# Row sums of the masked exponentials: from VectorE's mask to ScalarE's conversion

## The chip, the core and the metric

The kernel runs on one core of a Trainium2 chip. Its engines are TensorE (PE in the profile, with its weight loads as PEld), VectorE (DVE), ScalarE (ACT), GpSimd (POOL) and SyncE (SP), which issues most of the transfers. Each engine takes its instructions strictly in the order in which the program holds them, and waits in front of one until its semaphores allow it. The metric is the time of one execution in microseconds, as the median of several runs.

## The reference, cut to what matters

There are 4 batches of 576 tokens. Attention with 8 heads of 64 comes first: for each query only the 32 largest scores are kept, and the softmax is taken over those. After it stand a gated mixer and an FFN with a Fourier mix, both of width 512.

```python
scores = scale * np.matmul(q, k.transpose(0, 1, 3, 2))
kth = np.partition(scores, -32, axis=-1)[..., -32:-31]
scores = np.where(scores >= kth, scores, -1e9)
attn = np.exp(scores - np.max(scores, axis=-1, keepdims=True))
attn = attn / (np.sum(attn, axis=-1, keepdims=True) + 1e-09)
x = np.matmul(attn, v)                       # then heads side by side: [4, 576, 512]
val = (sigmoid(causal_conv(x, conv_w)) * (x @ w_val)) @ w_out
u = val + np.real(fft(fft(val, axis=1), axis=2))
out = u + np.maximum(layernorm(u) @ w_ch1, 0) @ w_ch2
```

The change touches `np.sum(attn)`: where the row sums of the 32 kept exponentials are added up.

## The kernel before, in words

**Attention.** The work is cut into 4 batches (blocks) of 4 head pairs, and each head pair into 5 tiles of queries: u = 0 to 3 hold 128 queries of both heads (two halves, i = 0 and 1), and u = 4 holds the last 64 queries of both heads in one half. That makes 80 tiles and 144 halves of 128 rows by 576 keys. For each tile PE makes the scores (`pss`, line 219), ACT copies them to SBUF (`ssb`, lines 220 and 221), and DVE finds the 32nd largest value of each row: it folds the row by maxima and minima (lines 245 to 249), then takes four rounds of MAX8 (line 260) over 96, 144, 288 and 576 columns, with MATCH_REPLACE8 (line 269) after each of the first three. ACT makes the exponentials `e` meanwhile (line 265).

**The mask.** `mask()` for a half is not run in its own tile but inside the next tile's sequence, between that tile's folds and its four rounds. On DVE one instruction (line 283) multiplies `e` by (score >= threshold) in place, and by `accum_out` also gives the row sum into a column of `sums`. Then ACT writes the fp16 high part of `e` into `hl` (line 284), POOL or (in block 0) PE and ACT make the low part (lines 285 to 292), SP issues a transposing DMA from `hl` to `et` (line 294), and PE multiplies `et` with the values into `pav` (line 316, 28 matmuls for a full tile). `hl` has two buffers and `et` four.

**The end of a head pair.** `attn_finish` turns the nine columns of `sums` into reciprocals `rs` (DVE lines 334 and 335), splits them into fp16 parts `rsh` (ACT line 337, POOL line 338), spreads them over a tile by 20 small matmuls (`pr` and `pt`, lines 345 and 350), copies that to `xt` (ACT lines 353 and 354) and multiplies `pav` by `xt` (DVE line 355). There are 16 head pairs.

**The other work.** While the attention of block b runs, the mixer and the FFN of block b - 1 run beside it as units (`moe_units`): `pv` (line 407) are the gate's value matmuls, `ph` (line 579) and `po` (lines 602 and 617) the two FFN layers. `po` of the last 64 tokens (line 617) is called po_4 below. The units of the last block have no attention beside them, and run after it. In block 0 the weights are unpacked instead (lines 671 to 699). The order on each engine is set by a planner: the program is written as one stream, and a simulated timeline with its own costs for every instruction decides which ready instruction comes next on each engine; scores and a few others have a higher priority. So a changed instruction shifts the order of others as well.

Of the kernel before, what the change touches and what calls it, by code (L numbers as in the profile page):

```python
# [12 lines left out]
AF = mybir.ActivationFunctionType  # L13
ALU = mybir.AluOpType
# [3 lines left out]
B, H, S, D = 4, 8, 576, 64  # L18
# [42 lines left out]
def mixer_pass(  # L61
# [17 lines left out]
    act = nc.scalar.activation  # L79
    vec = nc.vector  # L80
# [142 lines left out]
    def ordered(prev):  # L223
        if prev is None:
            return nullcontext()
        return tc.issue_after(prev.ins if hasattr(prev, "ins") else prev)

    def attn_tiles(b, hp, u):
        st = state[("at", b, hp)]
        g = 2 if u < 4 else 1  # L230
        cols = [u, 5 + u] if u < 4 else [4]
        sel = slice(u, u + 6, 5) if u < 4 else slice(4, 5)
        y = ap.tile([P, 2, S], F32, tag="ty", name=f"ty_{b}_{hp}_{u}", bufs=1)
        ngm = ap.tile([P, 2], F32, tag="ngm", name=f"ngm_{b}_{hp}_{u}", bufs=4)
        ssb, pss = st.pop(("s", u))
        c = st["c"]
        todo = deferred.pop("mask", [])
        last = deferred.get("last")

        if viol is not None:  # L240
            lo, hi = pss[:, :g, 0:HS], ssb[:, :g, HS:S]
            m2a = pss[:, 2, P : P + g * QS].rearrange("p (g n) -> p g n", g=g)
            m2b = y[:, :g, HS : HS + QS]
            with ordered(last):
                vec.tensor_tensor(m2a, lo[:, :, 0:QS], hi[:, :, 0:QS], op=ALU.max)
            vec.tensor_tensor(m2b, lo[:, :, QS:HS], hi[:, :, QS:HS], op=ALU.max)
            vec.tensor_tensor(y[:, :g, 0:QS], m2a, m2b, op=ALU.max)
            vec.tensor_tensor(y[:, :g, QS:HS], m2a, m2b, op=ALU.min)
            last = vec.tensor_tensor(y[:, :g, HS:S], lo, hi, op=ALU.min)  # L249
            rounds = ((y, slice(0, FS)), (y, slice(0, QS)), (y, slice(0, HS)), (y, slice(0, S)))  # L250
        else:
            al = slice(0, S)
            rounds = ((ssb, al), (y, al), (y, al), (y, al))
        for f in todo:
            last = f(last)
        es = []
        for r, (src, w) in enumerate(rounds):
            for i in range(g):
                with ordered(last):
                    last = vec.max(out=c[:, cols[i], 8 * r : 8 * r + 8], in_=src[:, i, w])  # L260
            if r == 0:
                nc.scalar.mul(ngm[:, :g], c[:, sel, 0:1].rearrange("p g n -> p (g n)"), -SC_EXP)
                for i in range(g):
                    e = ap.tile([P, S], F32, tag="e", name=f"e_{b}_{hp}_{u}_{i}", bufs=3)
                    act(e, ssb[:, i, :], AF.Exp, bias=ngm[:, i : i + 1], scale=SC_EXP)  # L265
                    es.append(e)
            if r < 3:
                for i in range(g):
                    vec.match_replace(  # L269
                        out=y[:, i, w],  # L270
                        in_to_replace=c[:, cols[i], 8 * r : 8 * r + 8],
                        in_values=src[:, i, w],
                        imm_value=-1e30,
                    )
        deferred["last"] = last

        def mask(i, prev):
            e = es[i]
            hl = ap.tile([P, 2 * S], F16, tag="hl", name=f"hl_{b}_{hp}_{u}_{i}", bufs=2)
            thr = c[:, cols[i], 31:32]  # L280
            rsum = st["sums"][:, cols[i] : cols[i] + 1]
            with ordered(prev):
                done = vec.scalar_tensor_tensor(e, ssb[:, i, :], thr, e, op0=ALU.is_ge, op1=ALU.mult, accum_out=rsum)  # L283
            act(hl[:, 0:S], e, AF.Copy, bias=0.0, scale=1.0)  # L284
            pool.tensor_tensor(hl[:, S : S + D], e[:, 512:S], hl[:, 512:S], op=ALU.subtract)  # L285
            if b == 0:
                pe = ps_m.tile([P, 512], F32, tag="psm", name=f"pe_{hp}_{u}_{i}")
                mm(pe, eye, e[:, 0:512], start=True, stop=False)  # L288
                mm(pe, neye, hl[:, 0:512], start=False, stop=True)
                act(hl[:, S + D : 2 * S], pe, AF.Copy, bias=0.0, scale=1.0)  # L290
            else:
                pool.tensor_tensor(hl[:, S + D : 2 * S], e[:, 0:512], hl[:, 0:512], op=ALU.subtract)  # L292
            et = ap.tile([P, 9, P], F16, tag="et", name=f"et_{b}_{hp}_{u}_{i}", bufs=4)
            nc.sync.dma_start_transpose(et, hl)
            st[("et", u, i)] = et
            if viol is not None and u == 4:
                vec.tensor_reduce(c[:, :, 0:1], c[:, :, 7:24:8], axis=mybir.AxisListType.X, op=ALU.min)
                vs = viol[:, b * NPAIR + hp]
                pool.tensor_tensor(vs, c[:, :, 31], c[:, :, 0], op=ALU.subtract)
            return done  # L300

        deferred["mask"] = [lambda prev, i=i: mask(i, prev) for i in range(g)]

    def attn_av(b, hp, u):
# [667 lines left out]
```

## Time and profile before

| what | us |
|---|---|
| median of 3 runs (1051.89 to 1061.42) | 1057.13 |
| the profiled execution, own time | 1057.91 |
| its span, first to last instruction | 1054.4 |

The profile is of one execution. Busy times are of instructions alone, and an engine's idle time is put down to what ended it. A row of the timeline can stand for several merged instructions (x2); then its length is that of all of them. Two neighbours on one engine overlap in the record: the next one begins some tens of ns before the record of the one ahead has ended, so the distance between two starts is what an instruction takes of its engine. A trace row names a tile without its buffer or index; in the order lists below, `pr_3_11979` is the tile pr of head pair 3 with a running number behind, `et_3_4_0` is of head pair 3, tile u = 4, half 0.

### The profile page before, as it was taken

The page shows a single profiled execution, that of the slowest core. Times are in us where ns is not written, and L with a number is a line of the kernel's source. Part 1 is how long each engine was busy: PE and PEld are TensorE (multiplying, and loading weights), DVE is VectorE, ACT ScalarE, POOL GpSimd, SP SyncE. Part 2 cuts the span into 40 slices and gives each one's busy share as a digit, 9 for nine tenths or more (in the row PEclk, how much of TensorE's full clock was granted, in tenths as well). Part 3 has the DMA queues.
Part 4 walks back from the last instruction along what each step waited for, and adds up shares of the span by engine and source line. Part 5 has one row for each costly group of instructions (what it writes and reads, how often), then busy time and mean ns, then how long its engine had stood idle before and what let it go on. Part 6 is the DMA issues. An engine that isn't in the chain of part 4 may idle for free.

```text
span 1054.4 us, 21240 instructions
## 1 busy us (share of the span) xinstructions
PE 881.2 (84%) x7282; PEld 513.4 (49%) x7282; DVE 846.2 (80%) x2568; ACT 664.3 (63%) x1394; POOL 565.4 (54%) x806
## 2 busy tenths in 40 slices
PE   1277767866789799898998998979979998899996
PEld 0033233322455565544656555446555564558563
DVE  5987979968898999998899998999998997223120
ACT  5587987868756877766669758565785763323020
POOL 1764652524485766755957658559584663641000
PEclk9977888988999999998999999999989999999999
DMA  7698585766536555555364546664464353301000
GB/s 205 162 269 222 128 189 129 181 109 131 103 63 105 97 113 120 100 125 123 82 122 93 116 97 110 138 141 70 99 111 91 83 108 55 80 21 26 21 2 29
DMA packets 308805, 115.18 MB, mean 109 GB/s; under 512 B 297040, under 2 KB 300880, under 8 KB 306384
## 3 DMA queue, kind: packets, MB, share of 16 engines
q1 hardware_dynamic: 303840, 90.24, 43.8%
q10 hardware_dynamic: 4848, 23.50, 6.8%
q8 instruction: 59, 0.97, 0.4%
q14 instruction: 58, 0.48, 0.2%
HBM read 44.49 MB, written 6.82 MB: 49 GB/s over the span
## 4 chain that ended last, share of the span: by engine, by line
DVE 32%; PE 27%; ACT 14%; DMA 12%; issue 6%; POOL 6%; SPq 2%; ACTq 0%; POOLq 0%; DVEq 0%
DVE e L283 7%; PE ph L579 6%; DMA et<-hl 5%; PE po L602 5%; DVE tc L260 5%; DVE ty L269 4%; PE pv L407 3%; DMA stk<-pre 3%; DVE ty L249 2%; POOL hl L292 2%; PE pav L316 2%; ACT hl L284 2%; ACT ssb L220 2%; ACT e L265 2%; PE pd L461 2%
## 5 line engine op out<-in xcount | busy, mean ns | idle before, releaser
L260 DVE MAX8 tc<-ty 128x8 f32<-128x96 f32 (+3 forms) x576 | 229.8, 432 | 2.5 <-DVE e L283 0.5
L579 PE MATMUL ph<-R_un,w 128*128 128x256 f16 (+1 forms) x1536 | 202.3, 290 | 14.0 <-ACT bx_h L583 6.5
L579 PEld LDWEIGHTS <-w 128*128 128x128 f16 x1536 | 148.4, 99 | 62.8 <-issue 21.0
L219 PE MATMUL pss<-stk 128*128 128x512 f16 (+3 forms) x640 | 95.0, 306 | 74.3 <-DVE ty L249 45.0
L284 ACT ACTIVATE hl<-e 128x576 f16<-128x576 f32 x144 | 97.9, 683 | 92.6 <-DVE e L283 70.0
L283 DVE SCALAR_TENSOR_TENSOR e<-ssb,tc,e 128x576 f32<-128x576 f32 x144 | 139.4, 996 | 2.6 <-ACT e L265 2.4
L269 DVE MATCH_REPLACE8 ty<-tc,ty 128x144 f32<-128x144 f32 (+2 forms) x432 | 137.2, 323 | 0.0
L602 PE MATMUL po<-w2f,bx_h 128*128 128x512 f16 x576 | 129.2, 379 | 0.0
L316 PE MATMUL pav<-et,vhl 128*64 128x128 f16 (+1 forms) x2240 | 95.2, 224 | 38.7 <-DMA et<-hl 36.9
L292 POOL TENSOR_TENSOR hl<-e,hl 128x512 f16<-128x512 f32 x108 | 125.0, 1157 | 0.0
L265 ACT ACTIVATE e<-ssb,ngm 128x576 f32<-128x576 f32 x144 | 107.4, 777 | 3.9 <-PE pe L288 1.4
L316 PEld LDWEIGHTS <-vhl 128*64 128x64 f16 x2240 | 72.1, 115 | 77.1 <-issue 72.7
L285 POOL TENSOR_TENSOR hl<-e,hl 128x64 f16<-128x64 f32 x144 | 47.5, 333 | 104.6 <-ACT hl L284 82.3
L163 POOL TENSOR_TENSOR pre<-r,pre 96x384 f16<-96x384 f32 x60 | 60.7, 1020 | 79.5 <-ACT r L162 66.8
L219 PEld LDWEIGHTS <-stk 128*128 128x128 f16 (+1 forms) x640 | 41.4, 104 | 124.3 <-issue 76.2
L602 PEld LDWEIGHTS <-bx_h 128*128 128x128 f16 x576 | 55.1, 98 | 64.9 <-issue 0.6
L220 ACT COPY ssb<-pss 128x1024 f32<-128x1024 f32 (+1 forms) x80 | 73.4, 918 | 10.4 <-PE pss L219 7.9
L580 ACT ACTIVATE bx_h<-ph 128x256 f16<-128x256 f32 (+1 forms) x96 | 38.7, 409 | 55.4 <-PE ph L579 55.2
L407 PE MATMUL pv<-xhl,R_wv 128*128 128x288 f16 x384 | 55.9, 303 | 13.1 <-ACT xt L353 5.0
L156 ACT ACTIVATE pre<-r 96x384 f16<-96x384 f32 x60 | 29.6, 519 | 44.6 <-DMA stk<-pre 16.5
L249 DVE TENSOR_TENSOR ty<-pss,ssb 128x576 f32<-128x576 f32 (+1 forms) x80 | 55.6, 695 | 1.9
L697 PE MATMUL pl<-bx_pre,U_wp 128*128 128x512 f32 x72 | 45.4, 716 | 12.0 <-ACT hl L290 6.4
(186 smaller groups left out, 1705.3 us busy)
## 6 DMA issues: line engine op xcount, KB each, us to landing
bx_pre<-in_moe_w_ch_dram ACTq DMA_DIRECT2D x8, 1024.0 KB, 5.7
bz_pre<-in_moe_w_ch_dram ACTq DMA_DIRECT2D x8, 1024.0 KB, 5.3
r<-in_q_dram SPq DMA_DIRECT2D x32, 144.0 KB, 2.7
r<-in_k_dram SPq DMA_DIRECT2D x31, 144.0 KB, 2.6
stk<-stk SPq DMA_DIRECT2D x60, 72.0 KB, 2.3
vr<-in_v_dram SPq DMA_DIRECT2D x32, 128.0 KB, 2.7
out_dram<-U_u SPq DMA_DIRECT2D x16, 256.0 KB, 2.4
R_wv<-scr_wv SPq DMA_DIRECT2D x3, 1024.0 KB, 5.1
```

The source lines that it names most:

```text
L219: mm(pss[pr, bank, cs], stk[:, 2 * vv, qs], stk[:, 1, ks], start=(vv == 0), stop=(vv == 1))
L220: nc.scalar.copy(ssb[:, :g, 0:512], pss[:, :g, :])
L260: last = vec.max(out=c[:, cols[i], 8 * r : 8 * r + 8], in_=src[:, i, w])
L265: act(e, ssb[:, i, :], AF.Exp, bias=ngm[:, i : i + 1], scale=SC_EXP)
L269: vec.match_replace(out=y[:, i, w], in_to_replace=c[:, cols[i], 8 * r : 8 * r + 8], in_values=src[:, i, w], imm_value=-1e30,)
L283: done = vec.scalar_tensor_tensor(e, ssb[:, i, :], thr, e, op0=ALU.is_ge, op1=ALU.mult, accum_out=rsum)
L284: act(hl[:, 0:S], e, AF.Copy, bias=0.0, scale=1.0)
L292: pool.tensor_tensor(hl[:, S + D : 2 * S], e[:, 0:512], hl[:, 0:512], op=ALU.subtract)
L316: av = mm(st["pav"][i * D : (i + 1) * D, qs], vhl[:, hv, i, cv, :], rhs, start=(m == 0), stop=(m == len(steps) - 1),)
L407: mm(pv[:, :HS], a, r, start=(n == 0), stop=(n == len(pairs) - 1))
L579: mm(ph[:, :nt], a, r, start=(i == 0), stop=(i == len(pr) - 1))
L602: mm(po, a, r, start=(f == 0 and i == 0), stop=(f == NF - 1 and i == 2))
```

## The change

The mask on DVE no longer has an accumulator output, and the conversion on ACT that follows it has one, into the same column of `sums`. What is summed is the same masked `e`. The line that reads `sums` (334) now waits for ACT.

```diff
             with ordered(prev):
-                done = vec.scalar_tensor_tensor(e, ssb[:, i, :], thr, e, op0=ALU.is_ge, op1=ALU.mult, accum_out=rsum)
-            act(hl[:, 0:S], e, AF.Copy, bias=0.0, scale=1.0)
+                done = vec.scalar_tensor_tensor(e, ssb[:, i, :], thr, e, op0=ALU.is_ge, op1=ALU.mult)
+            act(hl[:, 0:S], e, AF.Copy, bias=0.0, scale=1.0, accum_out=rsum)
             pool.tensor_tensor(hl[:, S : S + D], e[:, 512:S], hl[:, 512:S], op=ALU.subtract)
```

The order moves at many places. The first shown is DVE at the end of a head pair (block 1, head pair 1), from the mask of its last tile to the reciprocal. Before:

```order
L283 SCALAR_TENSOR_TENSOR e_1_4_0_4010,sums_1_2734<-ssb_1_4_3790,tc_1_2733,e_1_4_0_4010 128x576
L260 MAX tc_2_3643<-ty_2_0_4109 128x8 x2
L334 TENSOR_SCALAR rs_1_2735<-sums_1_2734 128x9
L269 MATCH_REPLACE ty_2_0_4109<-tc_2_3643,ty_2_0_4109 128x96 x2
L335 RECIPROCAL rs_1_2735<-rs_1_2735 128x9
L260 MAX tc_2_3643<-ty_2_0_4109 128x8 x2
```

and now:

```order
L283 SCALAR_TENSOR_TENSOR e_1_4_0_4010<-ssb_1_4_3790,tc_1_2733,e_1_4_0_4010 128x576
L260 MAX tc_2_3643<-ty_2_0_4109 128x8 x2
L269 MATCH_REPLACE ty_2_0_4109<-tc_2_3643,ty_2_0_4109 128x96 x2
L260 MAX tc_2_3643<-ty_2_0_4109 128x8
L334 TENSOR_SCALAR rs_1_2735<-sums_1_2734 128x9
L260 MAX tc_2_3643<-ty_2_0_4109 128x8
L269 MATCH_REPLACE ty_2_0_4109<-tc_2_3643,ty_2_0_4109 128x144
L335 RECIPROCAL rs_1_2735<-rs_1_2735 128x9
```

The line that reads the sums (334) has moved three instructions back, behind the second round's replacements and one MAX8 of 144 columns; the same move is made at most of the 16 head pairs.

The second place is PE at the end of the last head pair of block 3, where no more attention follows. Weight loads are left out, and of each run of matmuls into one tile the first stands. Before:

```order
L316 MATMUL pav_3_11702<-et_3_1_1_11642,vhl_3_10836 64x128
...
L345 MATMUL pr_3_11979<-neye,rsh_3_11976 64x128
...
L350 MATMUL pt_3_11996<-neye,rsh_3_11976 64x64
...
L617 MATMUL po_4_12015<-w2f,bx_h_10107 64x512
...
L316 MATMUL pav_3_11702<-et_3_2_0_11755,vhl_3_10836 64x128
...
L617 MATMUL po_4_12015<-w2f,bx_h_10107 64x512
...
L316 MATMUL pav_3_11702<-et_3_2_1_11762,vhl_3_10836 64x128
...
L617 MATMUL po_4_12015<-w2f,bx_h_10107 64x512
...
L316 MATMUL pav_3_11702<-et_3_3_0_11861,vhl_3_10836 64x128
...
L617 MATMUL po_4_12015<-w2f,bz_h_10457 64x512
...
L407 MATMUL pv_0_0_12074<-xhl_0_9997,R_wv_12068 128x288
```

and now:

```order
L316 MATMUL pav_3_11702<-et_3_1_0_11635,vhl_3_10836 64x128
...
L316 MATMUL pav_3_11702<-et_3_2_0_11755,vhl_3_10836 64x128
...
L316 MATMUL pav_3_11702<-et_3_3_0_11861,vhl_3_10836 64x128
...
L345 MATMUL pr_3_11979<-neye,rsh_3_11976 64x128
...
L350 MATMUL pt_3_11996<-neye,rsh_3_11976 64x64
...
L617 MATMUL po_4_12015<-w2f,bx_h_10107 64x512
...
L345 MATMUL pr_3_11979<-neye,rsh_3_11976 64x128
...
L316 MATMUL pav_3_11702<-et_3_4_0_11885,vhl_3_10836 64x64
...
L617 MATMUL po_4_12015<-w2f,bx_h_10107 64x512
...
L407 MATMUL pv_0_0_12074<-xhl_0_9997,R_wv_12068 128x288
```

Before, `pr` stood ahead of the last three tiles' `pav`, and the 48 matmuls of po_4 between them. Now the `pav` of u = 1, 2 and 3 come in one piece, `pr` behind them, then 9 matmuls of po_4, the rest of `pr`, the `pav` of u = 4, and only behind that the other 39 of po_4 and all 96 matmuls of `pv`. The first `pav` of this head pair now stands behind 37 matmuls of po_3 and not 44.

## Rows read from the trace of the kernel before

**Rows 1.** The page: busy time of the engines, and the chain that ended last by engine.

```profile
PE 881.2 (84%) x7282; PEld 513.4 (49%) x7282; DVE 846.2 (80%) x2568; ACT 664.3 (63%) x1394; POOL 565.4 (54%) x806
...
DVE 32%; PE 27%; ACT 14%; DMA 12%; issue 6%; POOL 6%; SPq 2%; ACTq 0%; POOLq 0%; DVEq 0%
```

**Rows 2.** Busy us by stretch: length, engines (instructions), clock, DMA share, GB/s.

```profile
750.00:850.00 100.00, 89.79 (x881) 57.74 (x879) 94.79 (x315) 73.48 (x172) 65.23 (x94) 0.97 0.50 94
850.00:890.00 40.00, 38.87 (x334) 21.65 (x333) 38.58 (x120) 22.14 (x49) 18.14 (x27) 1.00 0.32 73
...
960.00:1054.00 94.00, 86.44 (x555) 51.76 (x552) 16.61 (x35) 11.80 (x28) 1.75 (x3) 0.98 0.05 16
```

**Rows 3.** Groups by form on DVE: shapes, count | busy us, mean ns | idle.

```profile
L283 DVE SCALAR_TENSOR_TENSOR e<-ssb,tc,e 128x576 f32<-128x576 f32 x144 | 139.4, 996 | 2.6 <-ACT e L265 2.4
...
L369 DVE SCALAR_TENSOR_TENSOR e<-pav,cw,e 128x574 f32<-128x574 f32 x16 | 12.9, 804 | 0.1
...
L283 DVE DVE_READ_ACCUMULATOR e<-ssb,tc,e 128x1 f32 x144 | 11.5, 80 | 0.0
```

**Rows 4.** Instructions on DVE in order of time: start, length, engine, line, operation.

```profile
405.81 0.80 DVE L369 SCALAR_TENSOR_TENSOR e<-pav,cw,e 128x574 f32<-128x574 f32 x1
406.53 0.51 DVE L260 MAX8 tc<-ty 128x8 f32<-128x144 f32 x2
...
412.95 0.76 DVE L249 TENSOR_TENSOR ty<-pss,ssb 128x576 f32<-128x576 f32 x1
413.63 0.81 DVE L283 SCALAR_TENSOR_TENSOR e<-ssb,tc,e 128x576 f32<-128x576 f32 x1
414.36 0.08 DVE L283 DVE_READ_ACCUMULATOR e<-ssb,tc,e 128x1 f32 x1
414.36 0.82 DVE L283 SCALAR_TENSOR_TENSOR e<-ssb,tc,e 128x576 f32<-128x576 f32 x1
```

**Rows 5.** The conversion as a group by form on ACT.

```profile
L284 ACT ACTIVATE hl<-e 128x576 f16<-128x576 f32 x144 | 97.9, 683 | 92.6 <-DVE e L283 70.0 <-DMA et<-hl 19.1 <-DVE U_wp L759 1.8
```

**Rows 6.** Instructions on ACT in order of time, beside an accumulator read.

```profile
336.10 0.19 ACT L541 ACTIVATION_READ_ACCUMULATOR bz_u<-U_u,sm 128x1 f32 x1
336.19 0.76 ACT L265 ACTIVATE e<-ssb,ngm 128x576 f32<-128x576 f32 x1
```

**Rows 7.** Waits of DVE: who for whom, us in total, times, longest.

```profile
DVE pss L245 <- ACT ssb L221: 23.2, 18, 7.2
...
DVE bx_pre L671 <- PE pl L697: 15.9, 4, 7.4
```

**Rows 8.** Instructions on DVE and ACT at the end of a head pair, block 0.

```profile
273.85 0.81 DVE L283 SCALAR_TENSOR_TENSOR e<-ssb,tc,e 128x576 f32<-128x576 f32 x1
...
275.74 0.46 DVE L260 MAX8 tc<-ty 128x8 f32<-128x144 f32 x2
...
278.97 0.68 ACT L284 ACTIVATE hl<-e 128x576 f16<-128x576 f32 x1 [0.43 <-DMA et<-hl]
```

**Rows 9.** The same at the end of a head pair in block 1.

```profile
382.24 0.99 DVE L283 SCALAR_TENSOR_TENSOR e<-ssb,tc,e 128x576 f32<-128x576 f32 x1
...
384.32 0.46 DVE L260 MAX8 tc<-ty 128x8 f32<-128x144 f32 x2
...
385.00 0.68 ACT L284 ACTIVATE hl<-e 128x576 f16<-128x576 f32 x1 [1.96 <-DMA et<-hl]
```

**Rows 10.** Instructions on ACT and PE where the last attention tile ends.

```profile
899.56 0.68 ACT L284 ACTIVATE hl<-e 128x576 f16<-128x576 f32 x1 [4.12 <-DMA et<-hl]
...
877.75 7.93 PE L602 MATMUL po<-w2f,bx_h 128*128 128x512 f16 x36
...
890.74 1.27 PE L617 MATMUL po<-w2f,bx_h 128*64 128x512 f16 x10
...
905.08 0.63 PE L316 MATMUL pav<-et,vhl 128*64 128x64 f16 x28 [2.75 <-DMA et<-hl]
...
910.48 7.51 PE L407 MATMUL pv<-xhl,R_wv 128*128 128x288 f16 x60 [0.16 <-DVE e L408]
```

## The prediction

> **What bounds the kernel now.** I read the busy times and the chain that ended last first, then the stretches, then the groups of DVE and ACT, and last the order of time at the places where something is moved. DVE and PE carry the chain (32% and 27%) while ACT is busy 63% of the span [rows 1]. The stretches tell who bounds when: while attention runs, DVE is at 95 of 100 us, PE at 90, ACT at 73, and DVE still has 38.6 of the 40 us up to 890; in the last stretch PE is busy 86 of 94 us and DVE 17 [rows 2]. So a saving on DVE is worth its full size up to about 890 us of the span, and after that only what lets PE go on counts.
>
> **The change part by part.**
>
> *The mask loses its accumulator (DVE, 144 times).* The record shows the mask at 996 ns in the mean and behind each an accumulator read of 80 ns, 11.5 us in all [rows 3]. But the reader must look at starts, not lengths. The mask at 413.63 is followed by its read at 414.36, and the next mask starts at that same 414.36: the read lies wholly beside the next instruction. The mask takes 0.73 us of the engine from start to start; the nearest operation without accumulator, line 369 with the same kind of instruction and 574 columns, takes 0.72 (405.81 to 406.53) [rows 4], and undisturbed both have records of about 0.8 us. So the gain is 144 x 0.01 = 1.4 us. The lower bound is nothing. The upper one is the recorded 80 ns, plus a mask that becomes as quick as the TENSOR_TENSOR on 576 columns at 412.95, which takes 0.68 (412.95 to 413.63): 144 x (0.08 + 0.05) = 18.7 us. I take 1.4, because line 369 is the nearest row: same operation, same scalar from a pointer.
>
> The mask reads both tensors from SBUF, line 369 one of them from PSUM, and their slots are equal [rows 4]: a second source in SBUF costs the mask nothing that shows here. The Trainium skill, "Vector Engine (DVE) Microarchitecture Reference" (section 7, points that are easy to get wrong), says otherwise of this kind of instruction: with two such sources in SBUF it runs at half throughput, and no read port is left for the accumulator. If that hung on the accumulator, the mask would lose half of its time and the sum would be far below zero (a rival, below) and not above it; the equal slots speak against it.
>
> *The conversion gets one (ACT, 144 times).* Its group has 144 instructions of 683 ns [rows 5]. An accumulator read on ACT, as another line has it, is recorded with 0.19 us, but the next instruction starts 0.09 us after it (336.10, 336.19) [rows 6]. So ACT has 144 x 0.09 = 13 us more to do, about 1.6 us per 100, on 73: not a new bound. What it can cost is where DVE stands waiting for ACT: the copies of the scores end 18 waits of 23.2 us in all [rows 7]. With one read in front of each, 18 x 0.09 = 1.6 us. The bounds are 0 (the read falls into ACT's idle time) and 13 (every read on the path). I take 1.6, since ACT idles a quarter of that time. POOL and the transposing DMA get `hl` about 0.1 us later. Their consumer on PE runs two tiles behind, which hides it; without that cover the cost would sit in the 13.
>
> *The sums come from ACT, so line 334 waits (DVE, 16 times).* Before, it waited for DVE's own mask alone. Now DVE, which is in order, stands until the last conversion of the head pair and its accumulator read are done; behind it wait the rest of the next tile's rounds, and through them that tile's mask and everything downstream. The planner has moved the line back behind the second round's first MAX8. In block 0, head pair 3, that MAX8 pair starts at 275.74, so DVE reaches the line near 276.0; the conversion starts at 278.97, held by a DMA that has to free `hl`, and would be done at 278.97 + 0.68 + 0.09 = 279.7: a wait of 3.8 us [rows 8]. In block 1, head pair 1: DVE there near 384.5, sums at 385.00 + 0.77 = 385.8, a wait of 1.3 us [rows 9]. In most of the others the conversion follows its mask closely and the line finds it done. Two more waits of this sort lie early in block 0, where DVE later waits 15.9 us for PE's weight work in any case [rows 7]; I price those at nothing. Of the 5.1 us I take 3.5, because a DVE that is late finds the next score copies ready. The bounds: 0, if the transposes come earlier, and 10, if ACT now stands behind FFN work at other head pairs too.
>
> *The end of the attention (PE, once).* In the last head pair the sums come with the conversion at 899.56, near 900.4. DVE has nothing urgent behind line 334, since `pav` itself is only ready at 905.08 + 0.63 = 905.7 [rows 10], so that wait costs nothing. But the planner has put `pr`, which needs the sums, ahead of po_4 on PE, and so 39 of the 48 matmuls of po_4 no longer fill PE's waits for transposes; they come after the last `pav`. At 1.27 / 10 = 0.127 us each that is 5.0 us. Then all 96 `pv` at 7.51 / 60 = 0.125 follow: 12.0 us. So `pv` would end at 905.7 + 5.0 + 12.0 = 922.7 in place of 910.48 + 7.51 = 918.0, and PE bounds from there on: 4.7 us. Seven fewer matmuls of po_3 ahead of the first `pav`, at 7.93 / 36 = 0.22 each, let the transposes start up to 1.5 us earlier [rows 10]; I take half of it off, and 4.0 us. The bounds are 0 (something other than PE holds that stretch) and 6.
>
> *The rest of the order.* FFN units stand earlier against the attention tiles on DVE at many places. I find no row that prices this, so it is nothing in the sum, and 5 us either way in the range.
>
> **Sum.** -1.4 + 1.6 + 3.5 + 4.0 = +7.7 us. It is made against the profiled execution (1057.91 us, span 1054.4), which is 0.8 us above the median of the runs shown, 1057.13; from the median it gives 1064.8, and I predict **1065 us**, 0.7% slower.
>
> **The rivals.**
>
> *Faster: the accumulator read and a shorter mask come off DVE in full.* For it speaks that DVE is the bound for 890 us and that 11.5 us of reads are recorded [rows 3]; against it, that neighbours start together [rows 4]. It decides if masks without accumulator follow each other at clearly less than 0.73 us. Then -18.7, with line 334's waits hidden and the late po_4 kept (+4.0): 1042 us. An extreme of it: a mask without accumulator that takes half of its 0.73 us would give 144 x 0.36 = 52 us, and with the other terms 1057.1 - 52 + 9.1 = 1014 us; chance 0.02, because line 369 is no quicker without one. That is what the rule named above would come to.
>
> *No cost: the waits are hidden.* The planner moved line 334 back, transposes may come earlier, and the 39 matmuls may find idle time of PE. Then -1.4 + 1.6 and a remainder of the po_4 term: 1055 to 1060, say 1057 us. Against it stands the fixed order on PE.
>
> *Much slower: line 334 becomes a wait at most head pairs.* ACT's conversion may now stand behind FFN results that PE delivers late. With 13 head pairs outside the priced ones at 1 us each, 13 us on top: 1078 us. Against it: in the trace ACT has mostly waited for the mask (70.0 of the conversion's 92.6 us of idle) [rows 5], not the other way about.
>
> **How the numbers follow.** About 1% (10.6 us) is what a measurement of this kernel tells from no change: below 1046.6 is faster, above 1067.7 slower. Chances: forecast 0.46 (1058 to 1071), of which 0.17 lies over 1067.7; hidden 0.20; faster 0.17 (0.02 of it the extreme); much slower 0.17 (1071 to 1082). That makes 0.17 faster, 0.49 the same, 0.34 slower. A range of 1045 to 1077 leaves out most of the faster case and under half of the much slower one, 0.2 together, and takes in the 5 us for the order.
>
> **What would show it.** Right: masks on DVE still 0.73 us from start to start, no reads behind them; 144 reads on ACT with the next instruction 0.09 behind; a wait of line 334 for the conversion, 3 to 8 us in all; and a stretch from the last conversion (899.56 of 1054.4) to the end that is 4 us longer, with a long piece of po_4 behind the last `pav`. Wrong: masks closer together than 0.70 us (the faster case), no wait at line 334 (hidden), or more than 12 us of it (much slower).

## The result

The changed kernel takes 1047.1 us (median of 13 runs, 1039.8 to 1056.9) against 1057.1 us before (13 runs, 1050.6 to 1062.8). The ratio is **0.9914 [0.9884, 0.9943]**: 0.9% faster, where 0.7% slower was forecast. The ratio is of the means of the runs, without one slow run of the changed kernel (1056.9 us). The profiled execution took 1045.05 us, its span is 1042.8 us.

The page of the changed kernel, busy time of the engines, answers to [rows 1]:

```profile
PE 878.4 (84%) x7282; PEld 510.8 (49%) x7282; DVE 839.8 (81%) x2424; ACT 678.0 (65%) x1538; POOL 561.4 (54%) x806
```

DVE has 144 instructions fewer and ACT 144 more. DVE's groups by form (answer to [rows 3]; the accumulator read is gone), and ACT's two of line 284 (answer to [rows 5]):

```profile
L283 DVE SCALAR_TENSOR_TENSOR e<-ssb,tc,e 128x576 f32<-128x576 f32 x144 | 134.4, 967 | 3.7 <-ACT e L265 3.5
...
L369 DVE SCALAR_TENSOR_TENSOR e<-pav,cw,e 128x574 f32<-128x574 f32 x16 | 12.9, 804 | 0.1
```

```profile
L284 ACT ACTIVATE hl<-e 128x576 f16<-128x576 f32 x144 | 98.4, 684 | 76.8 <-DVE e L283 53.5 <-DMA et<-hl 13.9 <-issue 5.2
L284 ACT ACTIVATION_READ_ACCUMULATOR hl<-e 128x1 f32 x144 | 27.8, 193 | 0.0
```

Two masks and what follows them on DVE, and two conversions on ACT with their reads, in order of time (answers to [rows 4] and [rows 6]):

```profile
224.34 1.53 DVE L283 SCALAR_TENSOR_TENSOR e<-ssb,tc,e 128x576 f32<-128x576 f32 x2
225.79 0.41 DVE L260 MAX8 tc<-ty 128x8 f32<-128x96 f32 x2
```

```profile
208.74 0.67 ACT L284 ACTIVATE hl<-e 128x576 f16<-128x576 f32 x1
209.31 0.19 ACT L284 ACTIVATION_READ_ACCUMULATOR hl<-e 128x1 f32 x1
209.40 0.99 ACT L220 COPY ssb<-pss 128x1024 f32<-128x1024 f32 x1
```

Two masks take (225.79 - 224.34) / 2 = 0.725 us each from start to start, where one took 0.73 to 0.74 with its accumulator; the read on ACT takes 209.40 - 209.31 = 0.09 us. Both are as forecast. The new wait of line 334 came too, and is longer than forecast. DVE's waits (who for whom, us in total, times, longest; answer to [rows 7]), and below them line 453 in the kernel before:

```profile
DVE pss L245 <- ACT ssb L221: 24.5, 21, 7.3
DVE bx_y L453 <- ACT bx_y L452: 13.5, 5, 9.3
DVE rs L334 <- ACT hl L284: 13.0, 7, 2.8
DVE bx_pre L671 <- PE pl L697: 11.9, 2, 11.4
```

```profile
DVE bx_y L453 <- ACT bx_y L452: 17.3, 8, 9.1
```

13.0 us of waits at line 334, 2.3 of them behind the last mask. Yet DVE is idle 68.2 us between its first fold and the start of the last mask, and it was 69.1: the waits at lines 671 and 453 are shorter by as much (22.9 to 15.1 us in all at line 671, 17.3 to 13.5 at line 453).

**Where the 11.6 us of span went.** The last mask starts at 879.21 us instead of 887.27 (-8.1). From there to the end of the last `pv` it takes 27.0 us instead of 30.7 (-3.7). From there to the end they take 136.6 and 136.4 us. The end of the attention in the changed kernel, ACT, DVE and PE in order of time (answer to [rows 10]), and below it the last mask and the first `pav` of that head pair in the kernel before:

```profile
882.42 0.68 ACT L284 ACTIVATE hl<-e 128x576 f16<-128x576 f32 x1 [4.39 <-DMA et<-hl]
...
879.21 1.69 DVE L283 SCALAR_TENSOR_TENSOR e<-ssb,tc,e 128x576 f32<-128x576 f32 x1
883.23 0.17 DVE L334 TENSOR_SCALAR rs<-sums 128x9 f32<-128x9 f32 x1 [2.33 <-ACT hl L284]
...
871.11 0.97 PE L316 MATMUL pav<-et,vhl 128*64 128x128 f16 x28
874.50 1.27 PE L316 MATMUL pav<-et,vhl 128*64 128x128 f16 x29
...
885.59 2.34 PE L617 MATMUL po<-w2f,bx_h 128*64 128x512 f16 x9
...
888.79 0.94 PE L316 MATMUL pav<-et,vhl 128*64 128x64 f16 x28
889.80 1.92 PE L617 MATMUL po<-w2f,bx_h 128*64 128x512 f16 x16
...
894.24 11.93 PE L407 MATMUL pv<-xhl,R_wv 128*128 128x288 f16 x96
```

```profile
887.27 0.82 DVE L283 SCALAR_TENSOR_TENSOR e<-ssb,tc,e 128x576 f32<-128x576 f32 x1
...
887.34 0.97 PE L316 MATMUL pav<-et,vhl 128*64 128x128 f16 x28
```

The reader is to see two things. Only 9 matmuls of po_4 stand ahead of the `pav` of u = 4 (888.79), and between its end and the first `pv` lie 4.5 us of po_4, where the forecast had 5.0. But the head pair's first `pav` starts at 871.11, 8.1 us before the last mask. In the kernel before it started at 887.34, together with that mask, and the last conversion, which has to wait until `pav` frees `et` and the transposes free `hl`, came 12.3 us behind its mask (899.56); here it comes 3.2 us behind (882.42). The forecast had allowed up to 1.5 us for this. (po_3, which stands around these `pav`, is line 602 for the 128 tokens ahead of po_4's 64.)

### The profile page after: what moved, and what is told of

The parts are those of the page before. It is cut to its first block, busy times and chain, and to the rows that moved or that the text cites. A ratio compares the mean times of both kernels' runs of the same rounds, so it can differ in the third digit from the quotient of the medians.

```text
span 1042.8 us, 21245 instructions
## 1 busy us (share of the span) xinstructions
PE 878.4 (84%) x7282; PEld 510.8 (49%) x7282; DVE 839.8 (81%) x2424; ACT 678.0 (65%) x1538; POOL 561.4 (54%) x806
## 4 chain that ended last, share of the span: by engine, by line
PE 29%; DVE 15%; DMA 3%; ACT 3%; issue 2%; POOL 2%; SPq 1%; ACTq 0%; POOLq 0%; DVEq 0%
PE po L602 7%; PE ph L579 6%; DVE tc L260 4%; PE pu L497 3%; DVE ty L269 3%; DVE e L283 2%; PE pv L407 2%; PE pav L316 2%; PE pd L465 1%; PE pu L502 1%; PE pu L500 1%; PE pss L219 1%; DMA et<-hl 1%; PE pd L461 1%; PE po L617 1%
## 5 line engine op out<-in xcount | busy, mean ns | idle before, releaser
L579 PE MATMUL ph<-R_un,w 128*128 128x256 f16 (+1 forms) x1536 | 199.7, 288 | 10.9 <-ACT xt L353 4.2
L283 DVE SCALAR_TENSOR_TENSOR e<-ssb,tc,e 128x576 f32<-128x576 f32 x144 | 134.4, 967 | 3.7 <-ACT e L265 3.5
L316 PE MATMUL pav<-et,vhl 128*64 128x128 f16 (+1 forms) x2240 | 90.4, 221 | 41.2 <-DMA et<-hl 36.2
L245 DVE TENSOR_TENSOR pss<-pss,ssb 128x288 f32<-128x288 f32 (+1 forms) x80 | 33.7, 421 | 24.6 <-ACT ssb L221 24.5
```

Source lines behind the costliest of these rows:

```text
L316: av = mm(st["pav"][i * D : (i + 1) * D, qs], vhl[:, hv, i, cv, :], rhs, start=(m == 0), stop=(m == len(steps) - 1),)
L579: mm(ph[:, :nt], a, r, start=(i == 0), stop=(i == len(pr) - 1))
```

## The experiments

Ratios are against runs of the kernel before on the same chip, each with its 95% interval. Where a kernel's order on the engines is called that of another, the rows of all engines are the same (e13 has two more memsets on POOL at the start). Two theories: **order** (the planner's other order of instructions is what gains; the accumulator on DVE is nearly free) and **accumulator** (the mask became cheaper).

### The accumulator with the order held

```diff
 e1: the changed kernel with the accumulator back on DVE, scr: a scratch tile
-  ...scalar_tensor_tensor(e, ssb[:, i, :], thr, e, op0=ALU.is_ge, op1=ALU.mult)
+  ...scalar_tensor_tensor(e, ssb[:, i, :], thr, e, op0=..., op1=..., accum_out=st["scr"][:, cols[i] : cols[i] + 1])
 e13: the kernel before, accumulator only on a head pair's last mask
-  ..., accum_out=rsum)
+  ..., **({"accum_out": rsum} if u == 4 else {}))
```

> The changed kernel, with the mask's accumulator on DVE put back beside ACT's (it writes a scratch column that nobody reads); every engine issues its instructions in the order of the changed kernel. Theory order (the gain is the different order of instructions that the planner wrote for the changed kernel; the accumulator on DVE costs next to nothing): 1044 to 1049 us, ratio to before 0.988 to 0.993, mask records of 814 ns and 0.73 us from start to start as in the changed kernel. Theory accumulator (the mask is what became cheaper): 1054 to 1060 us, ratio 0.998 to 1.003.

Measured: **0.992 [0.988, 0.996]**, 1050.9 us: the ratio is where the order theory had it, the median 2 us above its range, and below that of the other theory.

> The kernel before with the mask's accumulator taken from 128 of its 144 masks (it stays on the one in a head pair's last tile), the row sums being left out (a constant stands for them); DVE, PE, ACT and SP issue exactly the rows of before in the order of before. If the accumulator by itself makes the mask cheaper, as between the two kernels without the timeline (4.4 us) and between the changed kernel and its twin with the accumulator (4.7 us less in masks in the profile): 3 to 5 us, 0.995 to 0.997, the masks taking 129 to 131 us instead of 133.7. If only the slot between two masks counts: 1.4 us, 0.998 to 0.999.

Measured: **1.0002 [0.9968, 1.0035]**. The masks take 132.8 us of DVE from start to start in all (133.7 before; in these sums the last mask is left out, and a mask with idle time behind it counts by its record), about 0.73 instead of 0.74 each. Their group:

```profile
L283 DVE SCALAR_TENSOR_TENSOR e<-ssb,tc,e 128x576 f32<-128x576 f32 x144 | 139.1, 998 | 2.6 <-ACT e L265 2.4
```

In the changed kernel's order the accumulator may come back and the gain stays; in the order of before it may go and there is none. The accumulator theory falls, and the larger of the two sizes that e13 allowed falls with it (0.995 to 0.997 was expected for it; the interval only touches that).

### One part of the change at a time

```diff
 e2: the kernel before without the accumulator on DVE
+  st["sums"]: pool.memset(st["sums"], 32.0);   line 334 issued behind the last mask
 e3: the kernel before with ACT's accumulator as well
-  act(hl[:, 0:S], e, AF.Copy, bias=0.0, scale=1.0)
+  act(hl[:, 0:S], e, AF.Copy, bias=0.0, scale=1.0, accum_out=st["scr"][:, cols[i] : cols[i] + 1])
 e4: the kernel before, line 334 issued behind the next tile's first MAX8 of round two
+  with ordered(second_round_max8): vec.tensor_scalar(rs[:, 0:9], sums[:, 0:9], ...)
```

> The kernel before with the mask's accumulator taken away and nothing on ACT instead: the row sums are left out (a constant that GpSimd fills once for each head pair stands for them), line 334 is issued behind the head pair's last mask as before, and the order of the engines stays close to that of before. Theory order: within 0.3% of before, 1054 to 1060 us. Theory accumulator: 0.985 to 0.993 of before, since the whole saving on DVE is there without the cost on ACT.

Measured: 0.9986 [0.9951, 1.0021].

> The kernel before with an accumulator on ACT's hi-part copy as well, into a scratch column that nobody reads; the sums still come from the mask on DVE. Theory order: the 144 reads on ACT cost 0 to 2 us, ratio 0.999 to 1.002, unless the order of DVE's work, which the planner shifts by a third of a tile in block 1, moves it: then up to 0.5% either way. Theory accumulator: 1.000 to 1.002, ACT not being the bound.

Measured: 1.0047 [1.0011, 1.0082]. Where it loses is not shown: its profiled execution, with 1055.8 us, lies 6.5 us under its median and so does not have the loss. In that profile DVE's waits for the score copies are 24.2 us, as in the changed kernel (24.5), and the masks take 144.4 us against 133.7, one of them 8.1 us long. More on such masks below.

> The kernel before with only line 334 (the first instruction on the row sums) moved behind the next tile's second-round MAX8 on DVE, as it stands in the changed kernel; sums from DVE, no accumulator on ACT. Theory order, with the shift of line 334 as its cause: 0.988 to 0.994 of before. Theory order, with the end of the attention and block 0's weight work as its causes: 0.998 to 1.003. Theory accumulator: 0.999 to 1.002.

Measured: 0.9976 [0.9934, 1.0017]. No part alone gives the gain. But each of the three brought an order of its own as well, which differs from that of before at hundreds of DVE's instructions, so they do not part the edit from the order as e1 and e13 do.

### The same cut in both kernels, which turns the orders about

```diff
 e5, e6: kernel before, changed kernel; from the 5th weight load on
-  nc.scalar.dma_start(raw, src)
+  nc.scalar.dma_start(raw[:, 0:256], src[:, 0:256])     # 2048 columns before; line 668 alike
```

> The kernel before with the weight loads of lines 668 and 670 cut to an eighth of their bytes from the fifth load on (16 of the 20 loads); the rest of those weights is left out, so the FFN works on stale numbers. The planner's order of DVE's other work against the attention tiles comes out 0.77 tile earlier in block 1 than in before (the changed kernel's was 0.38 tile earlier). Theory order: the waits at line 671 in block 0 (21.2 us) fall under 8 us, because the head pair's transposes no longer share the DMA engines with 1 MB loads, and block 1's earlier order gives 4 us more at the end: 0.978 to 0.988 of before. Theory accumulator: the loads alone, 0.985 to 0.995.

Measured: 0.9885 [0.984, 0.9929], 1045.1 us; DVE's idle time at line 671 fell from 22.9 to 6.0 us.

> The changed kernel with the same cut of the weight loads. Here the planner's order comes out 0.72 tile later in block 1 than in before. Theory order: the waits at line 671 fall as in the cut kernel before, but the later order of block 1 loses what the changed kernel had gained: 2 to 10 us slower than the cut kernel before, although its row sums come from ACT. Theory accumulator: 7 to 11 us faster than the cut kernel before.

Measured: **1.0004 [0.9972, 1.0037]**, 1056.8 us: 11.7 us slower than e5. The change makes the kernel slower by 1.1% where the planner happens to answer it with another order. Of the 12.4 us between the two spans 4.8 lie before the last mask, 8.9 between it and the end of `pv` (27.0 and 35.9 us; the first `pav` of the last head pair 3.5 us before the last mask in e5, with it in e6), and -1.2 behind. What costs the 4.8 is not shown: in e6 DVE's other work stands later in block 1, and the masks take 5.8 us more, one of them 8.3 us long. This is the plainest evidence for the order theory.

### Without the planner's timeline

```diff
 e7, e8, e9: kernel before, changed kernel, e1
-  with _tile.TileContext(nc, schedule_with_timeline_sim=True) as tc:
+  with _tile.TileContext(nc, schedule_with_timeline_sim=False) as tc:
```

> The kernel before with the planner's timeline off, so that instructions are put in order without its clock; the order then moves by about a tile against before, equally in this kernel and in the next one. Only the difference between the two counts; this one at 0.98 to 1.04 of before. Theory order: the next kernel within 0.4% of this one. Theory accumulator: the next kernel 7 to 11 us faster than this one.

> The changed kernel with the planner's timeline off; its order against the attention tiles is that of the kernel before without the timeline, to within a few hundredths of a tile (mean by block), save that line 334 stands later. Theory order: within 0.4% of the kernel before without the timeline: about 2 us saved at the mask, 2 to 6 us given back by line 334's waits for ACT. Theory accumulator: 7 to 11 us faster than that kernel.

> The changed kernel without the planner's timeline, with the mask's accumulator on DVE put back beside ACT's (into a scratch column that nobody reads); the order is exactly that of the changed kernel without the timeline (1186.8 us), which turned out to differ from that of the kernel before without it (1195.5 us) in 278 rows of DVE, in block 0 above all. Theory order: 1186 to 1190 us. Theory accumulator: 1193 to 1198 us.

Measured: 1195.5, 1186.8 and 1191.2 us (1.1328 [1.128, 1.1377], 1.1252 [1.1201, 1.1302], 1.1294 [1.1252, 1.1336]). e7 was expected at 0.98 to 1.04, and all three kernels are far slower than that. Against the order theory's expectation the changed one was 8.7 us faster than the one before. The mean shifts had hidden that the two orders differ: in 278 rows of DVE, mostly in block 0, where idle time at line 671 is 35.4 and 25.8 us. With one order (e8, e9) 4.4 us are left, between what the two theories had; the intervals of the two overlap, and e13 did not bear such a size out. This pair does not settle anything by itself.

### One unpacking moved

In the trace before, DVE stands 7.4 us at line 671 in block 0. PE, then DVE, at that place (first group), and PE and DVE of the changed kernel at the same step (second):

```profile
223.32 0.85 PE L316 MATMUL pav<-et,vhl 128*64 128x128 f16 x12 [7.11 <-DMA et<-hl]
228.06 1.13 PE L697 MATMUL pl<-bx_pre,U_wp 128*128 128x512 f32 x2
...
221.40 0.41 DVE L260 MAX8 tc<-ty 128x8 f32<-128x96 f32 x2
229.22 0.69 DVE L671 TENSOR_SCALAR bx_pre<-bz_pre 128x1024 int32<-128x1024 int32 x1 [7.41 <-PE pl L697]
```

```profile
220.01 0.63 PE L316 MATMUL pav<-et,vhl 128*64 128x128 f16 x15
222.48 1.12 PE L697 MATMUL pl<-bx_pre,U_wp 128*128 128x512 f32 x2
...
226.12 1.11 DVE L671 TENSOR_SCALAR bx_pre<-bz_pre 128x1024 int32<-128x1024 int32 x1
```

DVE waits for PE's `pl`, which stands in PE's queue behind a `pav` that waits 7.1 us for its transposed `et`; in the changed kernel `et` is there. That is a wait handed through three queues. The changed kernel pays elsewhere: 11.4 of its 15.1 us at line 671 are one wait earlier in block 0 (at 95.2 us), where the kernel before waits 3.3.

```diff
 e10: the kernel before
-  vec.tensor_scalar(ui, words[:, :, 1], 3, 0x40000000, ...)
+  with ordered(last_max8_of_tile_16 if load == 18 else None): vec.tensor_scalar(ui, words[:, :, 1], ...)
```

> The kernel before with one DVE instruction moved: the unpacking of the 18th weight load (line 671), which waited 7.4 us in tile 16 for PE's work on the load before it, is held until the tile's last MAX8. The order against the attention tiles stays that of before in blocks 1 and 2 (shifts of 0.02 and 0.04 tile). Theory order, with that wait as a part of the gain: tile 20 starts 3 to 8 us earlier than in before (271.3 us), and the whole is 0.993 to 0.998 of before. Theory that the wait is only moved on: tile 20 within 2 us of before, 0.998 to 1.003. Theory accumulator: 1.000, as the accumulator stays on DVE.

Measured: 1.0057 [1.0014, 1.01], outside all three. The wait is gone, and tile 20, the first of block 1, starts 2.4 us earlier (268.9), which is less than executions of one order differ by (the table below). What goes with the loss is another thing: in the profile (1068.4 us, 3 above the median) masks took 152.9 us, 19.2 more than before, and two of them 8.95 and 9.51. DVE and POOL in order of time at the first of these:

```profile
511.71 8.95 DVE L283 SCALAR_TENSOR_TENSOR e<-ssb,tc,e 128x576 f32<-128x576 f32 x1
520.59 0.81 DVE L283 SCALAR_TENSOR_TENSOR e<-ssb,tc,e 128x576 f32<-128x576 f32 x1
...
511.72 2.82 POOL L117 TENSOR_TENSOR bz_p<-bx_y,bz_p 128x290 f16<-128x290 f32 x4
514.50 5.54 POOL L117 TENSOR_TENSOR bx_y<-e,bx_y 128x288 f16<-128x288 f32 x8
```

The mask starts 0.01 us before a train of 12 subtractions on POOL and ends 0.6 us behind it (514.50 + 5.54 = 520.04, 520.66); the next mask takes 0.81. All 69 masks of 1.89 us and more in the twenty traces lie beside two-input instructions of POOL for two thirds of their length or more, and end 0.61 to 0.64 us after one of these has ended. Line 369, the same operation with one source in PSUM, keeps its 801 ns in this kernel too; 40 of its 52 instructions (of all lengths) lie beside POOL's for over half their time, and none takes more than 0.82 us:

```profile
L283 DVE SCALAR_TENSOR_TENSOR e<-ssb,tc,e 128x576 f32<-128x576 f32 x144 | 158.7, 1131 | 2.5 <-ACT e L265 2.4
...
L369 DVE SCALAR_TENSOR_TENSOR e<-pav,cw,e 128x574 f32<-128x574 f32 x16 | 12.8, 801 | 0.0
```

The Trainium skill, "SBUF — State Buffer" (who interferes with whom), says that a DVE instruction with two inputs in SBUF contends with a GpSimd instruction that reads SBUF. The same page of the Trainium skill (summary: rules for kernel authors) says that the second one to issue is blocked until the first has finished. The traces agree on who is held and who is not; that a mask is held through twelve instructions in a row goes beyond it.

### Pauses between POOL's pieces

```diff
 e14, e15: e10's kernel, the changed kernel; the same ahead of lines 416 and 417
-  cs = slice(i, min(i + w, n))
+  cs = slice(i, min(i + w, n)); pool.memset(gap, 0.0)
```

> The kernel with the one late unpacking (1.0057 of before, masks 152.9 us in all, two of them 8.95 and 9.50 us long beside trains of 12 GpSimd subtractions), with a tiny memset put on GpSimd between the pieces of these subtractions. Its order stays within 0.12 tile of that kernel. If DVE's mask is held for as long as GpSimd goes on without a pause: no mask over 3 us, masks under 138 us, 0.988 to 0.996 of before. If it is held by something else, or the memset makes no pause: two masks over 8 us again and 1.003 to 1.008.

Measured: 0.9964 [0.9928, 1.0]; masks 138.0 us, one still 8.13 us long. At that one the planner had put a single memset into the train and the other pieces in a row, so the pauses were not where they were meant to be, and the run does not tell what ends the hold. All that it shows is that masks shorter by 14.9 us, most of it the one long mask that is gone, go with 0.9% less time.

> The changed kernel with the same memsets between the pieces. Its masks took 127.1 us, the longest 1.97 us, so there is little left for a pause to save: 0 to 3 us from masks, against shifts of order in blocks 2 and 3 of a tenth of a tile: 0.987 to 0.993 of before. If the pauses are worth more than what the long masks show, under 0.985.

Measured: 0.9945 [0.9914, 0.9977], just above what was expected. Up to the last mask its profiled execution is 5.2 us ahead of the changed kernel, but its blocks 2 and 3 got the order in which the last head pair's first `pav` starts with the last mask: 34.4 us from there to the end of `pv`.

### The FFN stream earlier or later

```diff
 e11, e17: kernel before, 31.0 and 34.0.   e12, e16, e18: changed kernel, 31.0, 34.0 and 35.0
-  stream.append((36.0 * (b + 1) + LAG + acc / tot * (36.0 if b < B - 2 else 32.5), f))
+  stream.append((36.0 * (b + 1) + LAG + acc / tot * (36.0 if b < B - 2 else 34.0), f))
```

> The kernel before with block 2's FFN units spread over 31.0 instead of 32.5 steps of the attention, so that they are issued earlier; the order is the same until the last head pair. Theory order, with PE's lateness at the end as the other part of the gain: PE has its FFN rows done before the last mask, the last head pair's pav starts 4 to 8 us before the last mask instead of with it, from the last mask to the end of pv it takes 24 to 28 us instead of 30.7, and the whole is 0.993 to 0.998 of before. If that part is nothing: 0.999 to 1.002.

> The changed kernel with the same spread of 31.0 steps: in its order po_4 stands before the last pav and before pr, where the changed kernel has 39 of po_4's 48 matmuls behind it. Theory order: the 3 to 4 us that po_4 costs behind the last pav come back, 1041 to 1045 us, 0.985 to 0.989 of before. If PE is not late there: as the changed kernel, 0.991.

Measured: 1.0072 [1.0044, 1.01] and 0.9945 [0.9905, 0.9986]. Both expectations failed: 31.9 and 31.5 us from the last mask to the end of `pv`. But the place of `pav` is not what failed in e11: its first `pav` starts 2.4 us before the last mask (with it in the kernel before), and the last conversion stands 9.0 us behind that mask instead of 12.3. The gain is lost after that. POOL, SP and PE in e11, and POOL and SP in the kernel before:

```profile
898.92 1.15 POOL L292 TENSOR_TENSOR hl<-e,hl 128x512 f16<-128x512 f32 x1
...
900.31 0.34 SPq L387 DMA_DIRECT2D U_wp<-scr_wp  x1
900.83 1.42 SPq L294 DMA_TRANSPOSE et<-hl  x1
...
907.43 0.96 PE L316 MATMUL pav<-et,vhl 128*64 128x64 f16 x28 [5.43 <-DMA et<-hl]
```

```profile
900.59 1.16 POOL L292 TENSOR_TENSOR hl<-e,hl 128x512 f16<-128x512 f32 x1
...
901.77 1.62 SPq L294 DMA_TRANSPOSE et<-hl  x1
...
906.25 0.34 SPq L387 DMA_DIRECT2D U_wp<-scr_wp  x1
```

In e11 and e12, and in no other of the twenty traces, SP issues a weight load (line 387) directly ahead of the last transposing DMA. From the end of POOL's low part to the last `pav` it then takes 7.4 us (900.07 to 907.43), and 7.5 in e12, instead of 3.3 (901.75 to 905.08). That this load holds up the transpose is read from the order of the rows; no run moved it alone. In e12 the 3.3 us of po_4 came back as expected (13.1 us from the end of the last `pav` to that of `pv`, 16.4 in the changed kernel), but the first `pav` starts later than in the changed kernel (4.4 us before the last mask instead of 8.1), and the transpose takes 4 us more.

> The changed kernel with block 2's FFN units spread over 34.0 steps instead of 32.5, so that they are issued later; none of po_3's 48 matmuls stands ahead of the last head pair's first pav (37 do in the changed kernel), 24 ahead of the second, 43 ahead of the third. If only what stands ahead of that pav in PE's queue counts: last mask to the end of pv 22 to 25 us instead of 27.0, 0.986 to 0.990 of before. If the FFN rows that move behind count as much: 27 to 33 us, 0.991 to 0.997.

Measured: 0.9899 [0.9864, 0.9934], 25.7 us: the stretch lies between the two, the ratio in the first.

> The kernel before with block 2's FFN units spread over 34.0 steps instead of 32.5: 9 of po_3's 48 matmuls stand ahead of the last head pair's first pav (44 in before), 24 ahead of the second and third; nothing else moves before block 3. Theory order, with pav's place as the part at the end: the first pav starts 8 us or more before the last mask, last mask to the end of pv 25 to 28 us instead of 30.7 (30.7 to 30.9 in three more kernels with its order), 0.994 to 0.997 of before, without the change. If the end gained by something else in the change: 30 to 33 us, 0.999 to 1.003.

Measured: **0.9933 [0.9892, 0.9974]**, 23.5 us. The end of the attention in e17, ACT and PE:

```profile
892.54 0.68 ACT L284 ACTIVATE hl<-e 128x576 f16<-128x576 f32 x1 [3.31 <-DMA et<-hl]
...
879.51 0.30 PE L316 MATMUL pav<-et,vhl 128*64 128x128 f16 x3
880.91 3.41 PE L602 MATMUL po<-w2f,bx_h 128*128 128x512 f16 x15
884.25 1.02 PE L316 MATMUL pav<-et,vhl 128*64 128x128 f16 x29
...
898.05 0.71 PE L316 MATMUL pav<-et,vhl 128*64 128x64 f16 x26
```

The first `pav` starts 11.3 us before the last mask (890.8), the last conversion stands 1.7 us behind it instead of 12.3. So the gain at the end is had without the change, and is larger there.

> The changed kernel with 35.0 steps: 0, 12 and 37 of po_3's matmuls ahead of the last head pair's first three pav. If later goes on being better (31.5 us from the last mask to the end of pv at 31.0 steps, 27.0 at 32.5, 25.7 at 34.0): 24 to 25.5 us and 0.986 to 0.990 of before. If the FFN rows that fall behind the last pav take it back: 26 to 30 us and 0.990 to 0.994.

Measured: 0.9879 [0.983, 0.9928], 26.0 us to the end of `pv`: no better than 34.0 at the end, and the ratios of 32.5, 34.0 and 35.0 (0.9914, 0.9899, 0.9879) have intervals that overlap. e16 and e18 beat both kernels by their medians, 1041.9 and 1044.8 us; that they beat the changed one is not shown.

### The kernels of one order, side by side

Each row is one profile; within each half the orders are the same up to block 3. The start of tile 20 is the end of block 0. Masks are summed from start to start.

| kernel | start of tile 20 | DVE idle at line 671 | masks | last mask to end of pv |
|---|---|---|---|---|
| before | 271.3 | 22.9 | 133.7 | 30.7 |
| e13 | 260.7 | 13.0 | 132.8 | 30.9 |
| e11 | 268.2 | 20.9 | 134.0 | 31.9 |
| e17 | 274.8 | 27.9 | 133.1 | 23.5 |
| changed | 263.7 | 15.1 | 127.1 | 27.0 |
| e1 | 269.0 | 18.0 | 131.8 | 25.8 |
| e12 | 262.3 | 13.6 | 129.1 | 31.5 |
| e16 | 257.5 | 8.5 | 137.3 | 25.7 |
| e18 | 257.9 | 9.6 | 131.6 | 26.0 |

Within one order block 0 differs by up to 14 us in the first four rows and 11.5 in the last five. The masks differ too: the 77th, in block 2 and thus in one order in all five, takes 7.11 us in e16 and 0.91 in the other four. The means are 268.8 and 262.1 us for the start of tile 20, and 21.2 and 13.0 us at line 671: 7 and 8 us in favour of the changed order, about twice their standard errors (3.7 and 3.6). So the 7.6 us that the first two traces show in block 0 are likely, but one pair of traces could not have shown them.

## Why the prediction was wrong

- **The mask, -1.4 us: right.** 0.725 us from start to start for 0.73 to 0.74. e13 gives 0 with 3.5 us either way. The rule of half throughput that the prediction names, worked out to 1014 us, is not borne out: 128 masks without accumulator were not quicker.
- **ACT's reads, +1.6 us: right or too high.** 0.09 us each; DVE's waits for the score copies went from 23.2 to 24.5 us. e3, which has the reads alone, measured 1.0047, and no trace shows where that is lost.
- **Line 334, +3.5 us: the wait came, the cost did not.** 13.0 us, more than the 3 to 8 forecast, and by the forecast's own sign that would have meant the much slower rival. DVE as a whole was not idle for longer, since the waits at lines 671 and 453 were shorter. A wait was added to the sum as if the others stayed. e4 moved the line alone, without a wait for ACT, and measured 0.9976; no run has this wait in the order of before, so its own price is not shown.
- **The end of the attention, +4.0 us: one half right, one half mis-sized.** The late po_4 costs 4.1 us (12.3 to 16.4 us from the end of the last `pav` to that of `pv`), where 4.7 were forecast. But "let the transposes start up to 1.5 us earlier" was 7.9 us (last mask to the end of the last `pav`, 18.4 to 10.5 us). The rows priced only the seven matmuls of po_3 that changed places; that PE reached that place of its queue 16 us earlier, 8 of them against the last mask, was not in any of them. The term's sum is -3.7 instead of +4.0, and e17 shows that FFN rows moved behind `pav`, without the change, shorten that stretch by 7.2 us.
- **The rest of the order, "nothing in the sum, and 5 us either way": the step that failed.** The ratio's -9.1 us (of 1057.1) less the 3.7 at the end leaves about -5 us up to the last mask that no term of the sum held; five traces of the changed order against four make block 0 its likely place. And the end, too, was turned by the order. That 1047.1 us still lies inside the stated range is partly luck: the range allowed 5 us for the order, but not the turn at the end.
- **The rivals.** The faster one came near in its size and was wrong in its mechanism: the accumulator's part is 0. That the planner could place the last head pair otherwise was seen in the order and priced on one side only.

**Shown:** that the accumulator does not carry the gain (e1, e13), that the order decides the sign (e5, e6), that the place of the last head pair's `pav` against the FFN rows sets much of the end (e17; in e11 and e12 it is mixed with the late transpose, and e16 and e18 gain little more than the changed kernel). **Open:** how the -5 us before the last mask divide between waits in block 0 and masks held by POOL, since both move by more than that between executions; and why a hold ends behind one of POOL's instructions and not behind an earlier one. Freeing the last conversion by a third `hl` or a fifth `et` was not tried.

## What to carry to other kernels

Where a planner sets the order, a change of one instruction is a change of all of them: read from the new order where an engine reaches its next bottleneck, and give that a term with a sign, for it can be larger than everything the change was about. Before a gain is put down to the edit, undo the edit with the order held; here two runs did it, one in each order (e1, e13). And a matmul that frees a buffer for a transfer belongs ahead of work that nobody waits for, even if PE then has that work left over; what stands ahead of the transfer in the queue that issues it has to be looked at as well (e11, e12).

## What the runs showed of the hardware

- A DVE instruction with both sources in SBUF can be held by POOL's back-to-back subtractions for their whole train: 8.95 us for a mask of 0.81, with 12 instructions of 0.7 us beside it. In the sum over a kernel's masks that makes 127 to 153 us. It changes with the order, and in one order from one execution to the next: 7.11 us for a mask in e16 that takes 0.91 in the changed kernel.
- An accumulator on DVE's mask costs 0.01 us per instruction although its read has a record of its own of 80 ns, and one on ACT 0.09 us with a record of 193 ns.
- In one and the same order a wait in block 0 comes or does not: DVE's 7.4 us for the 18th weight load in the trace before was 0 in e13's and 5.4 in e17's.
